# Linear attention on one core: stores cut by partitions in five forms, and a longer warm-up

## The chip, the cores and the metric

One core of a Trainium2 chip runs the kernel. The metric is the device time of one execution in microseconds (us); lower is better. The kernel before takes 170.68 us, the median of three runs (170.63 to 170.9).

## What is computed

Linear attention with the feature map elu + 1, for 32 heads of 2048 positions and 128 dimensions, all in bf16:

```python
B, H, S, D = 1, 32, 2048, 128
phi_q = jnp.where(q > 0, q + 1, jnp.exp(q)) + 1e-6
phi_k = jnp.where(k > 0, k + 1, jnp.exp(k)) + 1e-6
kv = jnp.einsum("bhsd,bhse->bhde", phi_k, v)
z = jnp.einsum("bhsd->bhd", phi_k)
num = jnp.einsum("bhqd,bhde->bhqe", phi_q, kv)
den = jnp.einsum("bhqd,bhd->bhq", phi_q, z)[..., None] + 1e-6
return num / den
```

Each head reads q, k and v of 512 KB each and writes an output of 512 KB. Over 32 heads that is 50.33 MB read and 16.78 MB written.

## The kernel before, in words

**Tiling.** A head's 2048 positions lie over 128 partitions with 16 positions each: partition p holds positions 16p to 16p+15, 4 KB that are contiguous in memory (`rows`). Every load and every whole store is so one transfer of 128 rows of 4 KB; those of v are cut into 256 rows of 2 KB.

**One head.** The feature map is kept as a sum of two parts, min(exp(x), 1) + 1e-6 and max(x, 0). For k, ScalarE (ACT) takes exp (L328), VectorE (DVE) makes the first part (L334), GpSimd (POOL) the second (L330); for five of the sixteen tiles POOL adds both (L339). TensorE (PE) multiplies them with v and adds up kv and z in PSUM (L355, L277). q is first transposed on PE (L373), then goes through the same steps on ACT and DVE (L384, L387, L390, L393). PE multiplies phi_q with kv and z (L411, L417); DVE takes the reciprocal of the denominator (L456, L460) and divides into `o_sb` (L432, L438), with ACT's help in the last three heads (L447). From there a transfer stores it (L472).

**Buffers.** Inputs have six buffers each (NBI), outputs ten (NBO): the divide of head h+10 writes the buffer that the store of head h has read, and waits for that store to land. Each buffer has a semaphore of its own.

**What sets the order.** Every operation is given to a plan with its engine and a key, a number that tells how many heads in it is due; on each engine operations are issued in the order of their keys, and waits come from what they read and write. SyncE (SP) issues all transfers but the first v. Its order is that of the loads' keys (L320, h - 6.8 to h - 8) and the stores'. The stores' key grows faster than the heads do:

```python
late = h + 1.0 + 0.18 * h
for n, (t0, t1) in enumerate(PIECES.get(h, ((0, NT),))):
    store(t0, t1, late + 0.01 * n, bo if n == 0 else NBO + EXTRA[h] + n - 1)
```

So the store of head 0 has the key 1.0, that of head 20 the key 24.6 (L476), behind the last load's 24.2: the stores of heads 20 to 31 are all issued after the last load. Heads 0 to 29 are stored whole. The last two are cut by columns (tiles of a head, all 128 partitions): two pieces of 6 and 10 tiles (192 and 320 KB), and three of 6, 6 and 4 (192, 192 and 128 KB).

**The start.** Before its first data PE multiplies zeros: nine matmuls of 128x512 into three PSUM banks (`warm(9)`, L288 and L277, called at L296). PE's first real work, transposing q of head 0, waits for the third of the first transfers.

## Time and profile before

| what | before |
|---|---|
| median of three runs | 170.68 us (170.63 to 170.9) |
| the profiled execution's own time | 170.68 us |
| its span, first to last instruction | 168.8 us |
| granted TensorE clock, mean | 0.994 |
| transfers issued from SP | 130, and one from ACT |
| moved by DMA | 67.31 MB, 399 GB/s over the span |
| median time from issue to landing, whole store | 13.8 us |

The span is what the profile shows; the other 1.9 us lie around it. Busy times of engines and of the DMA queue can add to nearly the whole span at once, since all of them work side by side; which of them ends last is read from the stage in question. L numbers are lines of the kernel before. In the kernel after, lines behind the new constant are one or more higher: the whole store is then L473, the new cut one L482.

### The profile page before, as it was taken

The numbers are of one execution on the slowest core, as the hardware profiler recorded it, in microseconds if no ns is written. First come the engines' busy times: TensorE is split into PE (matmuls) and PEld (weight loads), VectorE is DVE, ScalarE is ACT, GpSimd is POOL, SyncE is SP. The second block draws the span as 40 slices with busy tenths as digits, with TensorE's granted clock in tenths as the row PEclk, the third lists the DMA queues.
The fourth block names the chain that finished last, engine by engine and source line by source line (L and its number), as shares of the span: only waits on it lengthen the run. The fifth ranks groups of instructions, "written<-read, shape, count | busy, mean of one in ns | idle before, by whom it ended". The sixth has DMA issues, their size and how long they took to land.

```text
span 168.8 us, 6570 instructions
## 1 busy us (share of the span) xinstructions
PE 158.0 (94%) x3089; PEld 151.7 (90%) x2401; DVE 149.6 (89%) x293; ACT 157.3 (93%) x180; POOL 105.5 (62%) x72
## 2 busy tenths in 40 slices
PE   7588999999999999999999999999999999999940
PEld 0488999999999999999999999999999999999830
DVE  0144999999999999999999999999999999999870
ACT  4599999999999999999999999999999999996960
POOL 3836866666677776666667776666667776666000
PEclk9999999999999999999999999999999999999997
DMA  5999999999999999999999999999999999999982
GB/s 204 412 414 411 412 406 409 406 415 408 411 414 409 415 416 415 418 413 419 415 414 415 416 413 420 413 419 415 413 416 418 417 414 415 411 413 415 412 333 104
DMA packets 22848, 67.31 MB, mean 399 GB/s; under 512 B 2097, under 2 KB 2609, under 8 KB 22833
## 3 DMA queue, kind: packets, MB, share of 16 engines
q1 hardware_dynamic: 22688, 66.59, 98.5%
q10 hardware_dynamic: 144, 0.52, 0.8%
q8 instruction: 9, 0.15, 0.3%
q14 instruction: 7, 0.05, 0.1%
HBM read 50.33 MB, written 16.78 MB: 398 GB/s over the span
## 4 chain that ended last, share of the span: by engine, by line
PE 87%; DMA 3%; DVE 3%; ACT 3%; issue 0%; SPq 0%
PE kvz_ps L355 36%; PE o_ps L411 32%; PE x_ps L373 16%; DMA q_sb<-in_q_dram 3%; DVE o_sb L438 1%; PE o_ps L277 1%; ACT eq_sb L384 1%; PE o_ps L417 1%; PE kvz_ps L277 1%; ACT ek_sb L328 1%; ACT rq_sb L387 1%; DVE emk_sb L334 0%; DVE rden_sb L460 0%; DVE den_sb L456 0%; SPq L320 0%
## 5 line engine op out<-in xcount | busy, mean ns | idle before, releaser
L384 ACT ACTIVATE eq_sb<-x_ps 128x1024 bf16<-128x1024 bf16 x64 | 72.4, 1349 | 3.4 <-PE x_ps L373 3.4
L339 POOL TENSOR_TENSOR rk_sb<-rk_sb,emk_sb 128x640 bf16<-128x640 bf16 x32 | 44.7, 1396 | 47.4 <-DVE emq_sb L393 41.2
L328 ACT ACTIVATE ek_sb<-k_sb 128x2048 bf16<-128x2048 bf16 x32 | 72.2, 2256 | 1.7 <-DMA k_sb<-in_k_dram 1.7
L438 DVE TENSOR_TENSOR o_sb<-o_ps,rden_sb 128x768 bf16<-128x768 f32 (+2 forms) x63 | 68.0, 1119 | 0.1
L355 PE MATMUL kvz_ps<-v_sb,rk_sb 128*128 128x128 bf16 (+1 forms) x512 | 67.6, 218 | 0.0
L330 POOL TENSOR_SCALAR rk_sb<-k_sb 128x2048 bf16<-128x2048 bf16 x32 | 60.6, 1892 | 2.7 <-DMA k_sb<-in_k_dram 2.0
L411 PE MATMUL o_ps<-kvs_sb,emq_sb 128*128 128x129 bf16 x474 | 60.6, 220 | 0.3 <-DVE o_sb L438 0.3
L411 PE MATMUL o_ps<-kvs_sb,rq_sb 128*128 128x129 bf16 x474 | 60.6, 220 | 0.0
L355 PE MATMUL kvz_ps<-v_sb,emk_sb 128*128 128x128 bf16 (+1 forms) x352 | 55.4, 219 | 1.2 <-DVE kvs_sb L365 1.2
L277 PE MATMUL kvz_ps<-ones_sb,rk_sb 128*128 128x1 bf16 x388 | 53.3, 166 | 0.0
L355 PEld LDWEIGHTS kvz_ps<-v_sb,rk_sb 128*128 128x128 bf16 x512 | 47.0, 97 | 1.5
L411 PEld LDWEIGHTS o_ps<-kvs_sb,rq_sb 128*128 128x128 bf16 x474 | 46.2, 97 | 0.0
L411 PEld LDWEIGHTS o_ps<-kvs_sb,emq_sb 128*128 128x128 bf16 x474 | 45.4, 97 | 0.6 <-DVE o_sb L438 0.4
L387 ACT ACTIVATE rq_sb<-x_ps 128x1024 bf16<-128x1024 bf16 x32 | 43.7, 1366 | 0.0
L277 PE MATMUL kvz_ps<-ones_sb,emk_sb 128*128 128x1 bf16 x228 | 37.8, 167 | 0.0
L373 PE MATMUL x_ps<-ident,q_sb 128*128 128x128 bf16 x512 | 34.6, 222 | 1.7 <-DMA q_sb<-in_q_dram 1.7
L373 PEld LDWEIGHTS x_ps<-ident,q_sb 128*128 128x128 bf16 x512 | 30.6, 99 | 5.6 <-DMA q_sb<-in_q_dram 5.6
L355 PEld LDWEIGHTS kvz_ps<-v_sb,emk_sb 128*128 128x128 bf16 x352 | 33.9, 97 | 1.5 <-issue 1.5
L334 DVE TENSOR_SCALAR emk_sb<-ek_sb 128x2048 bf16<-128x2048 bf16 x32 | 21.8, 682 | 8.8 <-ACT ek_sb L328 8.8
L390 DVE TENSOR_SCALAR rq_sb<-x_ps 128x1024 bf16<-128x1024 bf16 x32 | 21.8, 680 | 2.5 <-ACT eq_sb L384 2.5
L393 DVE TENSOR_SCALAR emq_sb<-eq_sb 128x2048 bf16<-128x2048 bf16 x32 | 22.1, 691 | 0.4 <-ACT eq_sb L384 0.4
L363 ACT ACTIVATE kvs_sb<-kvz_ps 128x128 bf16<-128x128 f32 x32 | 20.3, 634 | 0.0
(39 smaller groups left out, 78.2 us busy)
## 6 DMA issues: line engine op xcount, KB each, us to landing
k_sb<-in_k_dram SPq DMA_DIRECT2D x32, 512.0 KB, 13.2
q_sb<-in_q_dram SPq DMA_DIRECT2D x32, 512.0 KB, 13.2
v_sb<-in_v_dram SPq DMA_DIRECT2D x31, 512.0 KB, 13.6
out_dram<-o_sb SPq DMA_DIRECT2D x30, 512.0 KB, 13.8
out_dram<-o_sb SPq DMA_DIRECT2D x3, 192.0 KB, 4.7
v_sb<-in_v_dram ACTq DMA_DIRECT2D x1, 512.0 KB, 4.4
out_dram<-o_sb SPq DMA_DIRECT2D x1, 320.0 KB, 5.6
out_dram<-o_sb SPq DMA_DIRECT2D x1, 128.0 KB, 4.0
```

The lines of the kernel that those rows point to most:

```text
L277: return pe.add_instruction(mybir.InstMatmult(name=nc.get_next_instruction_name(), engine=mybir.EngineType.PE, ldweights=False, ins=[pe.lo ...
L328: lambda a, bi=bi, b2=b2: a.activation(ek_sb[:, b2, :], k_sb[:, bi, :], ACT.Exp),
L330: pl.add("pool", h, lambda g, bi=bi, b3=b3: g.tensor_scalar(rk_sb[:, b3, :], k_sb[:, bi, :], BIG, 0.0, op0=ALU.min, op1=ALU.max), reads=[( ...
L334: lambda d, b2=b2, b3=b3: d.tensor_scalar(emk_sb[:, b3, :], ek_sb[:, b2, :], 1.0, EPS, op0=ALU.min, op1=ALU.add),
L339: pl.add("pool", h + 0.5, lambda g, added=added: g.tensor_tensor(out=added(rk_sb), in0=added(rk_sb), in1=added(emk_sb), op=ALU.add), reads ...
L355: last = pe.matmul(kvz_ps[:, 1 - l:NC + r], lhsT=w, rhs=rhs, start=first, stop=fin, skip_group_check=True)
L373: last = pe.transpose(xT_ps[:, j * P:(j + 1) * P], q_sb[:, bi, j * P:(j + 1) * P], ident[:])
L384: lambda a, b2=b2, c=cols(half): a.activation(eq_sb[:, b2, c], xT_ps[:, c], ACT.Exp),
L387: lambda a, b3=b3, c=cols(1): a.activation(rq_sb[:, b3, c], xT_ps[:, c], ACT.Relu),
L393: lambda d, b2=b2, b3=b3: d.tensor_scalar(emq_sb[:, b3, :], eq_sb[:, b2, :], 1.0, EPS, op0=ALU.min, op1=ALU.add),
L411: last = pe.matmul(o_ap, lhsT=x[:, b3, t * P:(t + 1) * P], rhs=kvs_sb[:, b3, :], start=first, stop=not first)
L438: return lambda d: d.tensor_tensor(out=o_sb[:, bo, t0:t1, :].rearrange("p (a b) d -> p a b d", b=n), in0=_ap(nfull(b), 512 * b + NC * (t0 ...
```

## The change

A store of heads 0 to 29 takes one of five forms in turn, by the head's number: whole (h mod 5 = 0), or as two transfers that cut the 128 partitions into 64 and 64, 96 and 32, 32 and 96, or 16 and 112. Six heads take each form, so 24 heads have one transfer more. The two parts read the same buffer, follow each other in SP's order, and have a semaphore each; the divide ten heads later waits for both. The last two heads' pieces are as before. The warm-up has twelve matmuls in place of nine. On ACT, DVE, POOL and PE all else stays in its order.

```diff
+    PARTS = ((128,), (64, 64), (96, 32), (32, 96), (16, 112))
...
-        for n, c in (("k", NBI), ("q", NBI), ("v", NBI), ("o", NBO + 3), ("x", 1)):
+        for n, c in (("k", NBI), ("q", NBI), ("v", NBI), ("o", 2 * NBO + 3), ("x", 1)):
...
-        pl.add("pe", -9, warm(9), reads=[("warm",)], writes=[("banko", 2), ("banko", 3), ("banko", 4)])
+        pl.add("pe", -9, warm(12), reads=[("warm",)], writes=[("banko", 2), ("banko", 3), ("banko", 4)])
...
             late = h + 1.0 + 0.18 * h
+
+            if h not in PIECES and len(PARTS[h % len(PARTS)]) > 1:
+                r0 = 0
+                for n, r in enumerate(PARTS[h % len(PARTS)]):
+                    pl.add("sp", late + 0.01 * n, lambda sp, h=h, bo=bo, r0=r0, r=r: sp.dma_start(
+                        rows(of, h)[r0:r0 + r, :], o_sb[r0:r0 + r, bo].rearrange("p j d -> p (j d)")),
+                        reads=[("o", bo, t) for t in range(NT)], dma=("o", bo if n == 0 else NBO + 3 + bo))
+                    r0 += r
+                continue
             for n, (t0, t1) in enumerate(PIECES.get(h, ((0, NT),))):
                 store(t0, t1, late + 0.01 * n, bo if n == 0 else NBO + EXTRA[h] + n - 1)
```

## The prediction

> **What bounds the kernel now.** I read the page's first four parts, then the DMA queue's own waits, a table of windows, the DMA view of the last six microseconds, and the timeline of the start. The page, engines, slices and queues:

> ```profile
> PE 158.0 (94%) x3089; PEld 151.7 (90%) x2401; DVE 149.6 (89%) x293; ACT 157.3 (93%) x180; POOL 105.5 (62%) x72
> ...
> DMA  5999999999999999999999999999999999999982
> GB/s 204 412 414 411 412 406 409 406 415 408 411 414 409 415 416 415 418 413 419 415 414 415 416 413 420 413 419 415 413 416 418 417 414 415 411 413 415 412 333 104
> ...
> q1 hardware_dynamic: 22688, 66.59, 98.5%
> ```

> Two things are full at once: TensorE (94%) and the DMA engines, which move 406 to 420 GB/s from the second slice to the 38th. 512 KB, one whole transfer, take 1.26 us at 415 GB/s, and the trace's landing records show just that pace. The chain of waits gives PE 87%, because PE is never seen to wait; but the end is not PE's. The windows (columns: PE, PEld, DVE, ACT, POOL busy, granted clock, DMA share, GB/s):

> ```profile
> 100.00:140.00 40.00, 40.00 (x818) 39.62 (x636) 39.72 (x75) 40.00 (x45) 27.51 (x17) 1.00 1.03 415
> 140.00:152.00 12.00, 12.00 (x245) 11.88 (x191) 11.90 (x26) 12.00 (x13) 8.26 (x6) 1.00 1.04 414
> 152.00:160.00 8.00, 7.74 (x155) 7.35 (x119) 7.54 (x18) 6.52 (x15) 2.90 (x2) 1.00 1.02 413
> 160.00:164.00 4.00, 2.17 (x34) 1.88 (x32) 3.57 (x9) 3.22 (x12) 0.00 (x0) 1.00 0.89 357
> 164.00:168.80 4.80, 0.00 (x0) 0.00 (x0) 0.00 (x0) 0.00 (x0) 0.00 (x0) 0.80 0.32 119
> ```

> After 164 us no engine computes. What is left is a queue: the stores are placed ever later (the key of L476), the loads are all issued by 139.7 us, and from then on stores alone drain. The DMA view of 163 to 169 us (40 slices of 0.15 us):

> ```profile
> DMA  9666699861236999995111111100000000000000
> GB/s 403 256 270 273 263 389 410 355 222 58 99 116 249 399 393 342 342 379 191 65 38 55 48 41 51 41 31 21 31 20 24 20 21 0 0 0 0 0 0 0
> ```

> A full engine moves 415/16 = 26 GB/s. From 166.0 us on the rows read 65 to 38, then 31 to 20: **two engines, then one, finish alone**. The trace's landing records say the same: each transfer raises its semaphore sixteen times, once per engine, and for the last store fourteen of these come at 166.1 to 166.4 us, the fifteenth at 167.22, the last at 168.34. The end is the slowest DMA engine's.

> Why it is slow can be followed over the stores. From the landing of the last load (152.24 us) the next nine whole stores' last increments end at 164.58: 12.34/9 = 1.37 us each. Their first increments go from 148.70 to 159.95: 1.25 us each. In loads both advance alike (about 1.25). So one engine loses about 0.12 us on every whole store, on loads nothing; over 30 whole stores 3.6 us.

> **The change, part by part.**

> *The extra transfers.* Heads 0 to 29 are stored whole now; of these 24 (h mod 5 not 0) become two transfers, six heads in each split form. The bytes are the same; 24 more transfers are issued and 24 more completions counted. The nearest row is the end of this very trace: the last two heads go out as five transfers of 192, 320, 192, 192 and 128 KB, and their last increments run from 165.81 (the whole store before) to 168.34: 2.53 us for 1 MB, 1.265 per 512 KB. Cut in columns, with 128 partitions each, more transfers cost nothing. I take 0 for the number of transfers; the other end is 24 completions at the 9 ns that the trace's 4-byte packets took, 0.2 us per engine.

> *SP's issuing.* 24 more issues at 0.33 to 0.6 us (shortest and unblocked ones) are 8 to 14 us on SP. The views of the queue's line and waits:

> ```profile
> L472 SPq DMA_DIRECT2D out_dram<-o_sb x35: 332/1262/3232, 23.8 to 164.4; - x35
> ```

> ```profile
> SPq L472 <- DVE o_sb L438: 10.1, 7, 4.4
> ...
> SPq L152 <- DMA out_dram<-o_sb: 3.3, 4, 1.2
> ```

> The median issue lasts 1262 ns, the 1.26 us of one transfer: SP stands at a full queue, and from issue to landing 13 to 14 us pass. So longer issuing is covered by this backlog of some ten transfers; nothing. Both parts stand side by side in SP's order, no load comes between, and the second has no wait of its own. Without that cover it would be 8 to 14 us less of SP's idle time, and loads would come late.

> *The buffers.* The divide of head h+10 now waits for two landings instead of one. At head 28 (divided at about 151 us) store 18 has landed at 144.57; 6 us are left. Nothing.

> *Three more warm-up matmuls.* The timeline of the start:

> ```profile
> 1.39 3.62 PE L277 MATMUL o_ps<-warm_sb 128*128 128x512 bf16 x8
> ...
> 6.70 1.63 PEld L373 LDWEIGHTS x_ps<-ident,q_sb 128*128 128x128 bf16 x16 [5.62 <-DMA q_sb<-in_q_dram]
> 6.71 1.89 PE L373 MATMUL x_ps<-ident,q_sb 128*128 128x128 bf16 x16 [1.70 <-DMA q_sb<-in_q_dram]
> ```

> The eight start 0.43 us apart, so three more end 1.28 us later, at 6.3, and q lands at 6.66: hidden, with 0.4 us to spare; without that cover they would delay PE by up to 1.3 us. They may help: the first 16 transposes take 1.89 us, the next 16 (at 11.19) 1.05, so PE's first work could come up to 0.84 us earlier. But the DMA queue sets the end, and an earlier PE makes no byte move faster. I take 0, with +0.1 and -0.4 (a last issue at 164.0 in place of 164.38) as bounds.

> *What rows an engine gets.* Every transfer of this kernel has 128 partitions, so the price per split store is bounded from both sides. Below: the 0.12 us per store that the slowest engine loses go to other engines, if they belong to certain rows and not to that engine. Above: each part lasts as long as a whole, +1.26 us per split store. Of these I go by the nearer row, the five cut transfers that cost nothing, and by the slow engine: rows dealt in other ways over the engines move its handicap about. It would then be rid of 24 x 0.12 = 2.9 us, less its share of what is dealt out, 2.9/16 = 0.2. That is more than the 1.1 us by which it trails the fifteenth, so the fifteenth sets the end: 167.22 + 0.2 = 167.4 in place of 168.34, **-0.9 us**. PE's chain does not stop that: fourteen engines have landed the last store by 166.4.

> **Sum.** The profiled execution took 170.68 us, its span 168.8 and 1.9 around it; 170.68 is also the median of the runs. 170.68 + 0 + 0 + 0 + 0 - 0.9 = **169.8 us**, 0.5% less.

> [...]

> **Rivals.**

> [...]

> *The handicap is the engine's own.* Equal shares of bytes still go to each engine, the slow one stays slow, and splits cost nothing: 170.7 us (170.4 to 171.0). For it: only stores are slow there, which also fits an engine's way to memory.

> **How the numbers follow.** 0.2% (0.34 us) is about what a measurement of this kernel can tell from no change. Forecast 0.45, its own range 168.3 (both trailing engines relieved, 168.34 - 166.4 = 1.9 us, and the warm-up's 0.4) to 170.3 (0.4 gained). Handicap of the engine 0.12. Slower parts 0.43, spread over 171 to 189.6. The range is 168.4 to 183: above it lies about a third of the slow case, 0.16. Faster 0.45, same 0.12, slower 0.43.

> **What would show it.** Right: GB/s of 410 to 420 in all middle slices; the rows of one engine alone at the end shorter than 1 us; the last increments of split stores no longer 0.12 behind. Wrong: GB/s that dips wherever split stores drain, most in 141 to 164 us, where only stores are in the queue; waits of PE or ACT for DMA in mid-run; issues to landing longer than 13.8 us. The warm-up: transposes at 6.7 us taking about 1.05 us, and no earlier end. [...]

## The result, and the profile after

The kernel after takes **177.02 us**, the median of six runs (174.68 to 180.81), beside 170.63 (170.54 to 170.9) for the kernel before on the same chip. The ratio is 1.029, 95% interval 1.026 to 1.032; it leaves out the three slowest executions of the kernel after, which is why it lies below the ratio of the two medians. The time lies inside the predicted range (168.4 to 183), but on the other side: the forecast was 0.9 us faster, the kernel is about 5 us slower.

The profiled execution of the kernel after took 174.68 us, its span is 172.5. Its page, the same rows as before:

```profile
PE 159.2 (92%) x3092; PEld 151.7 (88%) x2401; DVE 150.2 (87%) x293; ACT 158.2 (92%) x180; POOL 105.6 (61%) x72
...
DMA  5999999999999999999999999999999999999875
GB/s 215 405 420 411 406 411 415 398 416 408 406 416 410 417 416 414 414 416 416 416 418 416 413 414 416 415 416 416 417 416 417 415 414 413 413 371 271 253 242 202
...
q1 hardware_dynamic: 23072, 66.59, 98.7%
```

The bytes are the same (66.59 MB in the queue), and up to the 35th slice the rate is what it was. The last five slices, 151 us to the end, read 371, 271, 253, 242 and 202, where before has 413, 415, 412, 333 and 104. The DMA row reads 9 through the first two of these: **the engines are busy there and move less**. The windows (columns: window, its length, busy time of PE, PEld, DVE, ACT and POOL, granted clock, DMA share, GB/s):

```profile
140.00:152.00 12.00, 12.00 (x243) 11.90 (x195) 11.90 (x26) 12.00 (x14) 7.58 (x6) 1.00 1.04 414
152.00:160.00 8.00, 8.00 (x168) 7.77 (x125) 7.54 (x17) 6.30 (x14) 3.71 (x3) 1.00 0.99 302
160.00:164.00 4.00, 2.72 (x44) 2.24 (x39) 3.59 (x13) 3.33 (x11) 0.00 (x0) 1.00 0.88 256
164.00:168.00 4.00, 0.00 (x0) 0.00 (x0) 0.78 (x1) 0.71 (x3) 0.00 (x0) 0.86 0.78 240
168.00:172.50 4.50, 0.00 (x0) 0.00 (x0) 0.00 (x0) 0.00 (x0) 0.00 (x0) 0.50 0.56 211
```

From 152 to 160 us the engines' share is 0.99, and 302 GB/s come of it, where before 1.02 gave 413. The packets say how: a row of 4 KB is one packet (12160 of 4096 bytes in either trace), and the trace has the time that each took. From 100 to 140 us their mean is 159 ns in both kernels. Of those that start from 152 to 160 us it is 161 ns before and 214 after, nine in ten up to 376 ns, the longest 1633. Only in this stage do packets take longer.

The boundary is sharp. The last load lands at 152.34 us (before 152.24). Before it the parts cost their bytes: by first increments the two halves of a 64 and 64 store near 130 us take 0.64 and 0.62 us, a 16 and 112 store near 120 us 0.18 and 1.09, where a whole store takes 1.25. Behind it, whole, 64/64 and 96/32 still follow each other at that pace, to 156.53 us; then the 32 and 96 store of head 23, whose parts land at 157.12 and 160.45, takes 3.9 us, and the engines spread. For one transfer, first and last increment lie 3.6 us apart at 152.34, 6.6 at 160.45, 8.4 at 164.78. SP stands longer at the full queue:

```profile
147.64 17.25 SPq L482 DMA_DIRECT2D out_dram<-o_sb  x8
164.99 4.38 SPq L473 DMA_DIRECT2D out_dram<-o_sb  x5
```

Eight issues of parts take 17.25 us, 2.2 each, though a part is on the mean half of 1.26 us of transfer.

The start, for the warm-up (start, duration):

```profile
1.39 4.90 PE L278 MATMUL o_ps<-warm_sb 128*128 128x512 bf16 x11
6.68 1.07 PE L374 MATMUL x_ps<-ident,q_sb 128*128 128x128 bf16 x16 [0.40 <-DMA q_sb<-in_q_dram]
```

The added matmuls end 0.40 us before q lands, and the first transposes take 1.07 us in place of 1.89.

### The profile page after: what moved, and what is told of

It reads as the page before. It is cut to its first block, busy times and chain, and to the rows that moved or that the text cites. A ratio compares the mean times of both kernels' runs of the same rounds, so it can differ in the third digit from the quotient of the medians.

```text
span 172.5 us, 6601 instructions
## 1 busy us (share of the span) xinstructions
PE 159.2 (92%) x3092; PEld 151.7 (88%) x2401; DVE 150.2 (87%) x293; ACT 158.2 (92%) x180; POOL 105.6 (61%) x72
## 3 DMA queue, kind: packets, MB, share of 16 engines
q1 hardware_dynamic: 23072, 66.59, 98.7%
## 4 chain that ended last, share of the span: by engine, by line
PE 84%; ACT 5%; DMA 3%; DVE 2%; issue 1%; SPq 0%
PE kvz_ps L356 34%; PE o_ps L412 31%; PE x_ps L374 16%; DMA q_sb<-in_q_dram 3%; ACT eq_sb L385 2%; DVE o_sb L439 1%; PE o_ps L278 1%; ACT ek_sb L329 1%; PE kvz_ps L278 1%; PE o_ps L418 1%; ACT o_sb L448 1%; ACT rq_sb L388 1%; DVE emk_sb L335 0%; DVE rden_sb L461 0%; SPq L321 0%
## 5 line engine op out<-in xcount | busy, mean ns | idle before, releaser
L356 PE MATMUL kvz_ps<-v_sb,rk_sb 128*128 128x128 bf16 (+1 forms) x512 | 68.3, 219 | 0.0
L385 ACT ACTIVATE eq_sb<-x_ps 128x1024 bf16<-128x1024 bf16 x64 | 62.1, 1022 | 3.4 <-PE x_ps L374 3.4
L329 ACT ACTIVATE ek_sb<-k_sb 128x2048 bf16<-128x2048 bf16 x32 | 61.9, 1934 | 1.7 <-DMA k_sb<-in_k_dram 1.7
L374 PEld LDWEIGHTS x_ps<-ident,q_sb 128*128 128x128 bf16 x512 | 29.9, 98 | 5.6 <-DMA q_sb<-in_q_dram 5.6
L374 PE MATMUL x_ps<-ident,q_sb 128*128 128x128 bf16 x512 | 33.8, 219 | 0.4 <-DMA q_sb<-in_q_dram 0.4
L388 ACT ACTIVATE rq_sb<-x_ps 128x1024 bf16<-128x1024 bf16 x32 | 33.1, 1033 | 0.0
L394 DVE TENSOR_SCALAR emq_sb<-eq_sb 128x2048 bf16<-128x2048 bf16 x32 | 22.6, 705 | 0.4 <-ACT eq_sb L385 0.4
L433 DVE TENSOR_TENSOR o_sb<-o_ps,rden_sb 128x128 bf16<-128x128 f32 x31 | 9.0, 291 | 1.0
```

The source lines that it names most:

```text
L329: lambda a, bi=bi, b2=b2: a.activation(ek_sb[:, b2, :], k_sb[:, bi, :], ACT.Exp),
L356: last = pe.matmul(kvz_ps[:, 1 - l:NC + r], lhsT=w, rhs=rhs, start=first, stop=fin, skip_group_check=True)
L374: last = pe.transpose(xT_ps[:, j * P:(j + 1) * P], q_sb[:, bi, j * P:(j + 1) * P], ident[:])
L385: lambda a, b2=b2, c=cols(half): a.activation(eq_sb[:, b2, c], xT_ps[:, c], ACT.Exp),
L388: lambda a, b3=b3, c=cols(1): a.activation(rq_sb[:, b3, c], xT_ps[:, c], ACT.Relu),
L394: lambda d, b2=b2, b3=b3: d.tensor_scalar(emq_sb[:, b3, :], eq_sb[:, b2, :], 1.0, EPS, op0=ALU.min, op1=ALU.add),
```

## The experiments

**Which part of the change costs.** Two theories stood at first: M, that cut stores cost only where *different* cuts are in flight one right behind another; and P, the prediction's slower parts, that a cut transfer is slower wherever it runs. M is Theory A of the expectations below; Theory B is a third, that the longer warm-up costs through PE's clock. Four kernels take the change apart. The first has the warm-up alone:

```diff
-        pl.add("pe", -9, warm(9), ...
+        pl.add("pe", -9, warm(12), ...
```

> The kernel before with twelve warm-up matmuls in place of nine, all stores as before. Theory A (the loss comes from stores of different cuts that drain one behind another at the end): the DMA queue sets the end, so 170.2 to 170.9 us, although PE is at half clock from about 13.2 to 16.7 us and ends about 0.8 us later. Theory B (the warm-up's dip of the clock makes a good part of the loss): 171.5 us or more, the span longer by the 0.8 us or more that PE is late.

Measured: 170.77 us, ratio 1.0001 (0.9991 to 1.0012). The warm-up does nothing to the time. The second has the five forms alone, with nine warm-up matmuls:

> The changed kernel with nine warm-up matmuls as before: only the five forms of stores. Theory A: 174 to 177 us, nearly all of the loss, with GB/s of 230 to 380 from 152 us on and 410 and more before. Theory B: under 173 us.

Measured: 176.66 us, ratio 1.035 (1.032 to 1.038): the whole loss is the forms'. The next two have them in one stage only, heads 0 to 19 (16 cut stores, between loads) or heads 20 to 29 (eight cut stores, all behind the last load):

```diff
-            if h not in PIECES and len(PARTS[h % len(PARTS)]) > 1:
+            if h < 20 and len(PARTS[h % len(PARTS)]) > 1:              # one kernel
+            if 20 <= h < NH - 2 and len(PARTS[h % len(PARTS)]) > 1:    # the other
```

> Five forms for heads 0 to 19 alone, whose stores stand between loads in the queue; heads 20 to 29 are stored whole; nine warm-up matmuls. Theory A: nothing is lost where loads stand between two stores, 170.4 to 170.9 us, as before. Rival (each cut store costs something wherever it stands): 16 of the 24 cut stores are in, so two thirds of the loss, 173 to 175 us.

> Five forms for heads 20 to 29 alone, whose stores follow one another without loads between; heads 0 to 19 whole; nine warm-up matmuls. Theory A: all of the loss with eight cut stores, 174 to 177 us. Rival (each cut store costs): a third of the loss, 172 us.

Measured: 170.91 us for the first, ratio 1.0012 (1.0002 to 1.0022), and 175.67 for the second, 1.026 (1.022 to 1.031). The page's rate rows, the first kernel and then the second:

```profile
GB/s 205 409 417 413 407 410 409 403 412 412 409 413 409 415 415 415 416 414 418 416 413 415 414 415 418 413 417 416 414 416 417 417 412 414 413 414 417 410 324 102
```

```profile
GB/s 212 409 420 408 409 411 412 403 412 411 411 413 414 419 415 413 419 412 415 417 415 418 413 418 414 416 418 413 417 417 416 415 412 415 409 305 271 210 278 105
```

Sixteen cut stores between loads show nowhere; eight among stores alone bring back the dip of the kernel after. P, a price per cut store wherever it runs, has fallen. The two stages do not add up to the whole, though: sixteen cut stores cost 0.1%, eight 2.6%, all 24 together 3.5%, and the kernel after with the same 24 cost 2.9%. Why the 24 cost more than the eight, no run shows. What is left is whether the stage makes any cut store dear, or only the mixture.

**One form, or a mixture.** The ten stores of heads 20 to 29 in one and the same form:

```diff
-    PARTS = ((128,), (64, 64), (96, 32), (32, 96), (16, 112))
+    PARTS = ((64, 64),)      # or ((96, 32),), or ((16, 112),)
```

> Heads 20 to 29, whose stores follow one another, all cut into 64 and 64 partitions; all else as in the kernel before. Theory M (engines that are apart by a store or more meet only because neighbouring stores deal the rows to the engines in different ways; one cut for all keeps each engine on its own rows): 170.4 to 171.5 us, 4 KB packets of 159 ns in the drain. [...]

> Heads 20 to 29 all cut into 96 and 32 partitions; all else as before. Theory M: 170.4 to 171.5 us. [...]

> All ten stores of heads 20 to 29 as 16 and 112 partitions, the most uneven form, the rest whole. Theory, only different cuts in flight together cost: 170.7 to 171.4 us, as with ten of 64 and 64 or ten of 96 and 32, packets near 159 ns. Rival, the most uneven form costs by itself (an engine gets one row, then seven): 172 us or more, 350 GB/s or less in 152 to 160 us.

Measured: 170.99 us (ratio 1.0015, 1.0004 to 1.0026), 171.04 (1.0028, 1.0012 to 1.0043) and 170.92 (1.0010, 0.9999 to 1.0022). Each has ten cut stores, two more than the kernel that lost 2.6%. The windows of the 64 and 64 kernel, and of the 16 and 112 one:

```profile
152.00:160.00 8.00, 7.68 (x152) 7.33 (x122) 7.48 (x20) 6.52 (x16) 2.50 (x2) 1.00 1.03 412
160.00:164.00 4.00, 1.82 (x31) 1.49 (x26) 3.22 (x8) 2.81 (x11) 0.00 (x0) 1.00 1.01 365
```

```profile
152.00:160.00 8.00, 7.68 (x151) 7.35 (x121) 7.48 (x20) 6.46 (x17) 2.35 (x2) 1.00 1.03 409
160.00:164.00 4.00, 1.67 (x28) 1.33 (x23) 3.07 (x8) 2.66 (x10) 0.00 (x0) 1.00 0.93 320
```

412 and 409 GB/s, with 4 KB packets of 162 ns on the mean in both from 152 to 160 us: none of these three forms costs by itself. The fifth, 32 and 96, was not run alone; it is 96 and 32 turned round, but that it is free behind the last load is not shown. From 160 us on the packets grow (182 and 189 ns): there the last cut stores stand next to the whole-height pieces of the last two heads, the one mixture that these kernels have left. Next, cut and whole stores by turns:

```diff
+    PARTS = ((128,), (64, 64))
```

> Heads 20 to 29 alternate whole (even) and 64 and 64 partitions (odd); all else as before. Each form by itself is free in the drain, so theory M (what costs is that neighbouring stores deal the rows differently) expects 172 to 175 us with two forms alone, packets over 300 ns from 152 us on. If it takes the uneven cuts or five forms to make engines meet: 170.5 to 171.3 us.

Measured: 172.86 us, ratio 1.009 (1.005 to 1.012), over runs from 170.86 to 174.0. The window of its profiled execution (173.35 us):

```profile
152.00:160.00 8.00, 7.68 (x151) 7.35 (x122) 7.48 (x20) 6.52 (x17) 2.23 (x2) 1.00 1.02 373
```

Five cut stores among five whole ones cost more than ten cut ones. Both forms are free by themselves, so here the mixture alone is left as the cause. The effect is smaller than that of five forms and varies from run to run, and the packets were expected at over 300 ns: their means are 177 and 203 ns in the two windows of the table below. Then two transfers per store without any cut in partitions, two column halves of 128 partitions each:

```diff
+            if 20 <= h < NH - 2:
+                store(0, NT // 2, late, bo)
+                store(NT // 2, NT, late + 0.01, NBO + 3 + bo)
```

> Heads 20 to 29 stored as two transfers each, cut by columns (8 tiles and 8 tiles, 2 KB runs, all 128 partitions in both); all else as before. [...] Rival (the number of transfers and completions in the drain is what costs): 174 us or more.

Measured: 171.28 us, ratio 1.0029 (1.0009 to 1.0049). Two transfers in place of one cost at most half a per cent.

**Which side of the transfer costs.** A transfer reads partitions and writes rows of the output; both change with the form. The first try shifted the output places of whole stores and left out the store of head 20:

```diff
...
+                base = 16 * (20 * P + 140 * (h - 21))
...
```

> All stores whole, but those of heads 21 to 29 go to places in the output that lie 140 blocks of 4 KB apart in place of 128, so that an engine writes other places within each 512 KB from head to head; the store of head 20 is left out to make room (1.26 us less to move), and heads 20 to 29 of the output are not in their places. If engines meet on the memory side of the store: 172 us or more, long packets from 152 us on. If they meet on the side of the partitions: 169.0 to 170.0 us, packets of 159 ns.

Measured: 169.47 us, ratio 0.993 (0.991 to 0.995), which is the 1.26 us of the store left out; packets of 161 ns. A shift harms nothing, but it is a weak mixture. Two later kernels separate the sides: one has the five forms in the partitions read, while the parts' rows are placed so that each sixteenth, counted in order, writes the same output rows in every form; the other stores whole and transposes the output rows within the head by turns.

```diff
...
-                        rows(of, h)[r0:r0 + r, :], o_sb[r0:r0 + r, bo]...
+                        rows(of, h).rearrange("(e i) x -> e i x", i=8)[:, r0 // 16:(r0 + r) // 16, :], o_sb[r0:r0 + r, bo]...
```

> The kernel that uses the five forms for heads 20 to 29 only, with one edit: the parts' rows go to other places of the same head's output, so that sixteenth e of a part and sixteenth e of the other part together write the output rows 8e to 8e+7, as in a whole store. If each engine takes one sixteenth of a transfer's rows in order, it writes in every form the same eight rows of a head; only the partitions that it reads differ from form to form. (Rows within heads 20 to 29 are permuted in the output.) Theory, partitions' side: the mixture still costs as in the drain-only kernel, 174 to 177 us, 300 GB/s or so in 152 to 160 us, 4 KB packets well over 159 ns on the mean. Rival, memory's side: nothing is mixed any more, 170.5 to 171.2 us, 410 GB/s in 152 to 160 us, packets of 159 ns.

```diff
...
+                c = (1, 8, 4, 2, 8)[h % 5]
...
+                    rows(of, h).rearrange("(c e) x -> e c x", c=c), o_sb[:, bo]...
```

> [...] (Rows within heads 20 to 29 are permuted in the output.) Theory, partitions' side: nothing is mixed on that side, 170.5 to 171.2 us, packets of 159 ns, 410 GB/s in 152 to 160 us. Rival, memory's side: the engines meet on the output rows, 172 us or more, with packets longer than 159 ns on the mean from 152 us on.

Measured: partitions mixed, 175.87 us, ratio 1.026 (1.023 to 1.030), the same ratio as that of the eight cut stores with both sides mixed. Rows mixed, 172.37 us, ratio 1.010 (1.008 to 1.012). The windows of the first (its profiled execution took 176.85 us, the second longest of six from 174.15 to 177.38) and of the second:

```profile
152.00:160.00 8.00, 7.68 (x151) 7.33 (x121) 7.48 (x20) 6.52 (x16) 2.48 (x2) 1.00 0.98 294
160.00:164.00 4.00, 1.79 (x31) 1.47 (x26) 3.20 (x8) 2.79 (x10) 0.00 (x0) 1.00 0.63 177
```

```profile
152.00:160.00 8.00, 8.00 (x166) 7.79 (x124) 7.55 (x18) 6.52 (x14) 3.35 (x3) 1.00 1.01 385
160.00:164.00 4.00, 2.35 (x38) 1.87 (x32) 3.59 (x11) 3.33 (x13) 0.00 (x0) 1.00 0.84 283
```

The placing of the rows rests on an assumption that no record shows, that an engine takes its sixteenth of a transfer's rows in order; under it, mixing the partitions alone brings the full loss. But the expectation for mixed rows, 170.5 to 171.2, was missed too: that side is not free. One more kernel has the same transposed order in all ten stores:

```diff
-                c = (1, 8, 4, 2, 8)[h % 5]
+                c = 8
```

> As the kernel with transposed output rows, but all ten stores of heads 20 to 29 in one and the same turn (partition 8e+c to row 16c+e), with no store in order between them. (Rows within heads 20 to 29 are permuted in the output.) If mixing is what costs, on whichever side: 170.5 to 171.3 us and packets near 159 ns from 152 us on, save where the last two heads' pieces meet the last of them. If the transposed shape costs by itself: 172 us or more, as with the shapes in turns.

Measured: 170.78 us, ratio 0.9999 (0.9990 to 1.0008). Again the shape is free and the mixture is not.

**Does it need stores?** Loads of q of the odd heads cut 64 and 64, between the whole loads of k and v, all stores as before:

```diff
+                if name == "q" and h % 2:
+                    for n in (0, 1):
+                        pl.add("sp", key + 0.001 * n, ... sp.dma_start(dst[64 * n:64 * n + 64], rws[64 * n:64 * n + 64]), ...
```

> The same question for loads: the q of every odd head is loaded as 64 and 64 partitions, between whole loads of k and v; stores as before, nine warm-up matmuls. If a mixture of deals holds up the write side of the partitions as it does the read side, the whole run slows down, since mixed loads are in flight from the start and the engines are 1.6 us and more apart from 19 us on: 175 us or more, long 4 KB packets all along. If only reads of the partitions (stores) meet: 170.5 to 171.2 us.

Measured: 198.39 us, ratio 1.162 (1.160 to 1.164). The page, and two of its waits (engine, line, what was waited for: us in total, times, longest):

```profile
DMA  6999999999999999999999999999999999999993
GB/s 246 334 406 320 372 313 359 290 399 339 376 383 310 415 283 389 361 307 386 318 416 280 397 358 305 361 304 414 305 372 354 306 367 313 364 321 401 399 360 117
```

```profile
PE x_ps L378 <- DMA q_sb<-in_q_dram: 9.6, 7, 1.9
PE kvz_ps L360 <- DMA v_sb<-in_v_dram: 4.2, 6, 1.0
```

The engines are busy all the time and the rate swings between 280 and 416; packets take 187 ns on the mean from 100 to 140 us. Sixteen cut loads of 96 lose nearly 28 us: here loads of both cuts follow each other the whole run long, and now PE waits for data.

This is not the mixture alone, for a cut load costs by itself. The first one, of head 1, runs with the engines nearly in step (first and last increment 0.8 us apart). By first increments its halves take 1.19 and 1.11 us, where the same load whole takes 1.23 in the kernel before; 4 KB packets from 7.5 to 8.3 us take 272 ns on the mean, before 159. The windows of this kernel and of the kernel before:

```profile
7.30:9.60 2.30, 2.30 (x38) 2.28 (x19) 1.16 (x2) 2.30 (x3) 2.30 (x2) 0.53 1.02 248
```

```profile
7.30:9.60 2.30, 2.30 (x31) 2.24 (x20) 0.69 (x1) 1.82 (x2) 2.30 (x2) 1.00 1.01 405
```

Each half takes nearly as long as a whole. A cut store does not: that of head 1 in the kernel after lands from 42.36 us on, twelve of its sixteen increments within 0.52 us, and its halves take 0.65 and 0.63 us. Later, with the engines of the load kernel 5.6 us apart (first increments at 91.59 and 92.39 us), the halves of a cut load take 0.62 and 0.79 us, and the whole load behind them 2.05 in place of 1.3: there the whole neighbours pay. No run has all loads cut alike, so how much of the 16% is the mixture's stays open.

**Can the slow engine be relieved?** The prediction's gain hung on the slowest DMA engine. In the landing record of head 8's store, cut into 120 and 8 partitions, one increment comes right after the issue, at 74.4 us, and fifteen from 83.5 us on, when data land. Read as fifteen engines with data and one without, that leaves an engine out; if it were the slow one, its handicap would shrink. For head 8, and for heads 6 and 12:

```diff
+    PARTS = ((120, 8),)
-            if 20 <= h < NH - 2 and len(PARTS[h % len(PARTS)]) > 1:
+            if len(PARTS[0]) > 1 and h in (8,):      # or (6, 12)
```

> The kernel before with the store of head 8 alone, between loads, cut into 120 and 8 partitions. 120 is not a multiple of sixteen but of fifteen: should fifteen engines share the first part and eight the second, the last engine has no part of this store, 32 KB or 1.25 to 1.38 us less, and eight engines have 4 KB or 0.16 us more. If the engine that is slow on stores is that one, the end comes when the fifteenth is done: 1.1 us earlier less 0.2, 169.7 to 170.1 us. If it is another one: 170.7 to 171.0 us.

> The same with two stores, of heads 6 and 12, cut into 120 and 8: the last engine has 2.5 us or more less to do, eight engines 0.3 us more. If the slow engine is the one left out: 169.5 to 170.0 us, hardly better than with one, since another engine sets the end. If not: 170.8 to 171.2 us.

Measured: 170.87 us, ratio 1.0006 (0.9996 to 1.0016), and 171.04, 1.0022 (1.0013 to 1.0032). No gain. The engine left out is not the slow one, or what it is spared doesn't reach the end. No version that stores everything beat the kernel before.

Ratios, and the mean ns of the 4 KB packets that start in two windows of each profiled execution:

| kernel | ratio | 152 to 160 us | 160 to 172 us |
|---|---|---|---|
| before | 1 | 161 | 160 |
| after | 1.029 | 214 | 220 |
| five forms, heads 0 to 19 | 1.001 | 161 | 160 |
| five forms, heads 20 to 29 | 1.026 | 214 | 244 |
| all 64/64 | 1.002 | 162 | 182 |
| all 96/32 | 1.003 | 163 | 186 |
| all 16/112 | 1.001 | 162 | 189 |
| whole and 64/64 by turns | 1.009 | 177 | 203 |
| partitions mixed, rows as in whole stores | 1.026 | 216 | 237 |
| rows mixed, partitions as in whole stores | 1.010 | 171 | 193 |
| rows transposed, all alike | 1.000 | 161 | 174 |

**What follows.** For stores M stands: whole and 64/64 are each free behind the last load and cost 0.9% by turns, and one transposed order of the rows is free throughout, while several in turns cost 1%. How much of the five forms' loss is the mixture's and how much, if any, belongs to 32 and 96 was not separated. A reading that fits the rows of the stores, the author's estimate and shown by no record: a transfer lands in sixteen increments, each part of a cut store too; take these as one per engine, with a sixteenth of the rows each, and let it depend on the form which rows they are. With one form throughout, a partition would then always fall to the same engine, and engines that drift apart would not meet on it. With another form it would fall to another engine; that would hurt only when engines stand in different transfers at once. Between loads two stores are some 5 us apart and the engines 2.6 to 3.5, so they don't; behind the last load a store follows every 1.26 us, and an engine 3.6 us ahead is two or three stores further on. There packets take longer (214 ns in place of 161), the spread grows (from 3.6 to 8.4 us), and more engines would meet. That the stores must stand close together, with no loads between, is shown (1.001 against 1.026). That mixing the partitions alone is enough for the whole loss is not: it holds only if an engine takes its sixteenth in order, which was not seen directly (the records name no partition), nor what the engines would meet on. Open, too, is how much of the 1% of the mixed rows is the memory's: if the transposed stores were dealt to the engines otherwise than in order, their partitions were mixed as well. And the reading does not cover the loads: by it nothing within one cut load makes engines meet, and with the engines 0.8 us apart its halves still took 1.19 and 1.11 us, little more than half the pace.

## Why the prediction was wrong

- **What bounds the kernel** was right: the queue of stores behind the last load sets the end, and all that was lost was lost there.
- **The extra transfers** at 0: right. Sixteen between loads cost 0.12%, ten in the drain 0.1 to 0.3%.
- **SP's issuing and the buffers** at 0: right. Only the window after 152 us changed; whole stores still land a median 14.0 us after issue (13.8 before).
- **The warm-up** at 0 with transposes of 1.05 us: right, 1.07 and a ratio of 1.0001.
- **"What rows an engine gets"** is the step that failed, and twice over. It stood in the sum at -0.9 us; the five forms by themselves cost 3.5%, about 6 us, and the kernel after about 5. First, its gain: I took it that the 0.12 us of the slowest engine belong to rows, and that a cut gives these to other engines; the records show no engine's rows. They belong to the engine, as far as the landing records tell. Near 130 us the last increment trails the first by another 0.06 us in each half of a 64 and 64 store; near 120 us by 0.03 in a 16 part and 0.15 in the 112 part. Had the loss belonged to certain rows, one half alone would have trailed; it goes roughly with the bytes, whichever rows they are. Second, its price: I bounded it per split store and went by the five column pieces at the end, which have 128 partitions each. They showed that *more* transfers are free, and I read them as if they showed that *other rows* are free. Nothing in the trace of before had two cuts in flight. In place of no price, stores of different forms close together cost each other: 4 KB packets of 214 ns in place of 161.
- **Slower parts**, at 0.43 and 171 to 189.6 us, had the right sign, and "most in 141 to 164 us, where only stores are in the queue" is nearly where the dip came: from 152 us on, since up to then the last loads were still landing (414 GB/s from 140 to 152 us). No run shows the price per cut store that this spread, and with it the range's upper end, is made of. What the runs showed in its place: 0.1 to 0.3% for ten stores in any of the three forms tried alone, 0.1% for sixteen cut stores between loads, 2.6% for eight in mixed forms behind the last load. Nor did it help that the engines were apart there: by the reading above, their spread is what makes stores of different forms collide. A load, which the change left whole, paid less at the front with the engines apart (0.62 and 0.79 us for its halves) than with the engines in step (1.19 and 1.11).
- **The upper bound per split store**, each part as long as a whole (+1.26 us), is far off for stores: 0.64 and 0.62 us for two parts of 256 KB, and ten 64 and 64 stores in a row at 412 GB/s. The first cut load comes near it: 1.19 and 1.11 us. No run isolates one half moving alone.
- **The engine's own handicap**, the rival at 0.12, fits the landing records (0.06 us in each half); its time, 170.4 to 171.0 us, is that of the five forms in heads 0 to 19 (170.91).

## What to carry to other kernels

Cutting a store by partitions was neither dear nor a gain here (0.1 to 0.3% for ten in one form); cutting neighbours differently was dear (2.6% for eight). Where stores stand back to back at the full rate, give them all the same partitions in the same order. Leave loads whole: cutting one in six cost 16%, and part of that was the cut's own price. In a profile, look for a DMA share near 1 with a rate below the steady one, and for longer packets: here 0.99 at 302 GB/s, with packets of 214 ns in place of 161, was stores of different cuts back to back, not a queue that ran empty.

## What the runs showed of the hardware that was not expected

```profile
9.90:13.20 3.30, 1.17 (x23) 1.00 (x18) 1.57 (x4) 3.30 (x5) 0.43 (x2) 1.00 1.03 423
13.20:16.70 3.50, 3.50 (x51) 3.37 (x30) 1.39 (x2) 3.50 (x5) 2.79 (x2) 0.51 1.03 408
```

PE had been busy for 1.17 of 3.3 us just before. The clock's records put the start of full speed at 6.42 us and the half speed at 13.24 to 16.66 us, 3.41 us long. In the kernel with the warm-up alone PE is busy for the same 1.17 us from 9.90 to 13.20 us, and the granted clock stays at 1.00 from 13.20 to 16.70; its full speed starts at 5.15 us. What brought the half speed, no run shows.
